# Attention with eight tokens per partition, a list scheduler for the front, and block products for two more operands

## The chip, the cores and the metric

The kernel runs on one core of one Trainium2 chip. The metric is the device time of one execution in microseconds. The kernel before took 1674.87 us (median of 3 runs, 1673.18 to 1677.12).

## The reference

Attention over q, k, v of shape (4, 8, 576, 64), batch, heads, tokens and head size, followed by a mixture of 8 experts over all 2304 tokens with 512 features.

```python
# attention, per batch and head; factor = 4
out_d  = softmax(scale * q_d @ k_d.T) @ v_d      # q_d, k_d, v_d: means over 4 neighbouring tokens (144 rows)
out_up = repeat(out_d, 4)                        # coarse part, repeated for the 4 tokens
mask   = |i - j| < 4                             # local part: 7 neighbours of every token
out    = out_up + softmax(where(mask, scale * q @ k.T, -1e9)) @ v
x      = out, heads side by side                 # (2304, 512)
# experts: every expert sees every token
P = exp(x @ w_gate - max); 8 rounds: rows / row sum, columns / column sum, * 2304 / 8
out = sum over e of P[:, e] * (relu(x @ w1[e]) @ w2[e])   # w1[e] (512, 1024), w2[e] (1024, 512)
```

## The kernel before

**Splitting of numbers.** All large products are made of numbers in two parts, high and low: a high part rounded by ScalarE and a low part, the remainder, by GpSimd or VectorE. A product of two such numbers is three matmuls (high by high, high by low, low by high). Weights arrive as raw tiles `r` of 128x512; `w_convert` (L193) turns each into `w1h`/`w1l` or `w2h`/`w2l`, at L204 and L211 or L214.

**Chunks and pieces.** Four neighbouring tokens are one group, and there are 576 groups. They are cut into six chunks of 64, 64, 128, 128, 128 and 64 groups (L49), that is 256 or 512 tokens. A *piece* is one chunk, or two small chunks side by side. `order` (L1031) lists pairs of a piece and an expert. Each pair has 8 units (`NF`); a unit is `mm1` (L976: 12 matmuls over the piece's tokens into `psh`, then relu into `hh` on ScalarE and the remainder `hl` on VectorE, L991 and L999) and `mm2` (L1004: three matmuls of 512 columns for each tile of 128 tokens into `psy`). The matmuls of the next unit's `mm1` stand ahead of the present unit's `mm2` in TensorE's order. Each unit loads two raw tiles of 256 KB anew.

**The start.** Until the first chunk's x exists, TensorE has no expert work. SyncE (SP) issues loads in a fixed order: q and key windows of the first attention unit (`l_load_q` L233, `l_load_win` L245), the coarse loads `dr` of keys (L423), value windows, `dr` of values, weights. A window holds for 4 tokens the 10 rows that they need; a partition holds one group of 4 tokens of four heads.

**Local attention.** `l_gen` (L276) works through nine units. A unit is 128 groups by four heads. For each head VectorE makes a product `prod` of q and window (L299), a sum over the head size (L322), the softmax over 7 scores (L335 to L355), a product of window and score (L366) and a sum over the window (L397) into `lo`. Three `lo` tiles rotate. For unit 1 alone the q operand and the scores stand in PSUM (`qp`, `scp`); for the others all operands stand in SBUF. In the first unit GpSimd makes five of the eight products.

**Coarse attention.** For the batches after the first, `d_load` reads q, k, v once more, GpSimd sums four tokens (`p_gen` L449, at L473 and L477), and `d_gen` (L627) makes the two products and the softmax for each half of the heads, one after another. `x_gen` (L781) transposes `lo`, adds the coarse output `od` and splits the sum into `xh` and `xl`. A chunk that crosses from one batch to the next needs the coarse output of both.

**The front.** The loop at L1153 places one unit after another, and between them `pump` (L958) places steps of four generators, by a simple clock of each engine: the main chain (`m_gen` L921: coarse attention, x, gate logits, then the gate's rounds `s_gen` L861, all in one chain), the coarse sums, and local attention. As the gate's weights are not known yet, each finished tile of the front is copied to DRAM (`spill`, L1181), and read back later.

**After the front.** The remaining pairs run at L1365, beside them the spilled tiles are read back and added (`back_add`), and `t_gen` (L1256) forms sums of x for the last part. That part handles chunks 3 and 4 (1024 tokens) of all experts by a block product: `m_pair` (L1458) makes a 2x2 block product from 7 products in place of 8. The block part covers `mm1`; its second product (`y_mm`, L1505) is as before. An expert is two halves, each of 84 matmuls in two calls of `m_pair` and 96 in `y_mm`, all of 512 columns.

Of the kernel before, what the change touches and what calls it, by code (L numbers as in the profile page):

```python
# [20 lines left out]
def attention_moe_kernel(  # L21
# [10 lines left out]
    nc = tc.nc  # L32
# [11 lines left out]
    WR = R + 2 * (R - 1)  # L44
# [4 lines left out]
    chunks = [(0, 64), (64, 64)] + [(128 + 128 * i, 128) for i in range(3)] + [(512, 64)]  # L49
# [18 lines left out]
    ps_a = ctx.enter_context(tc.tile_pool(name="ps_a", bufs=2, space=PSUM))  # L68
# [3 lines left out]
    ones = const.tile([128, 128], F32, name="ones")  # L72
    spill = dram.tile([32, 4, 128, DM], F32, name="spill")
# [27 lines left out]
    ap3 = att.enter_context(tc.tile_pool(name="ap3", bufs=3, side="right"))  # L101
    mask = ap1.tile([128, NC, R * W], F32, name="mask")
# [32 lines left out]
    clk = {"pe": 0.0, "dve": 0.0, "act": 0.0, "pool": 0.0, "dma": 0.0}  # L135
    HOP = 0.1

    def at(eng, cost, *deps):
        clk[eng] = max([clk[eng]] + [d + HOP for d in deps]) + cost
        return clk[eng]  # L140

    def dve(n, *deps):
        return at("dve", 0.07 + n / 960.0, *deps)

    def act(n, *deps):
        return at("act", 0.1 + n / 1200.0, *deps)

    def pool(n, *deps):
        return at("pool", 0.02 + n / 420.0, *deps)
# [4 lines left out]

    a_rel = []

    def pa():
        i = len(a_rel)
        a_rel.append(0.0)
        return i, (a_rel[i - 2] if i >= 2 else 0.0)  # L160

    def dma(kb, *deps):

        return at("dma", 0.05 + kb * 0.55, *deps) + 2.0
# [6 lines left out]
    n_dma = [0]  # L171
    n_cv = [0]
    free_t = {}

    def w_load():
        n = n_dma[0]
        if n >= len(units):
            return
        n_dma[0] += 1
        e, f, _ = units[n]  # L180
        r1 = rawp.tile([128, KD, 128], F32, tag="r", name="r1")
        r2 = rawp.tile([128, DM], F32, tag="r", name="r2")
        nc.sync.dma_start(  # L183
            out=r1, in_=moe_w1[e, :, f * 128:(f + 1) * 128].rearrange("(k p) f -> p k f", p=128)
        )
        nc.sync.dma_start(out=r2, in_=moe_w2[e, f * 128:(f + 1) * 128, :])  # L186
        w_raw[n] = (r1, r2, dma(4, clk["pe"], w_ready.get(n - NRAW, 0.0)))

    def w_can(limit, now):
        n = n_cv[0]  # L190
        return n < min(limit, len(units)) and w_raw[n][2] <= now + 0.2

    def w_convert(*deps, need=1e9, low2=nc.gpsimd):  # L193
        n = n_cv[0]
        n_cv[0] += 1
        r1, r2, t_raw = w_raw.pop(n)
        pl = units[n][2]()
        h1 = pl.tile([128, KD, 128], F32R, tag="w1h", name="w1h")
        l1 = pl.tile([128, KD, 128], F32R, tag="w1l", name="w1l")
        h2 = pl.tile([128, DM], F32R, tag="w2h", name="w2h")  # L200
        l2 = pl.tile([128, DM], F32R, tag="w2l", name="w2l")
        done = 0.0
        for r, h, l in ((r1, h1, l1), (r2, h2, l2)):
            nc.scalar.activation(out=h, in_=r, func=AF.Copy)  # L204
            t = act(512, t_raw, *deps)
            t_pool = max(clk["pool"], t) + 1.3
            if r is r2 and can("p", clk["pool"]):
                t_pool += 1
            t_dve = max(clk["dve"], t) + 0.6
            if low2 is nc.gpsimd if r is r2 else t_pool <= max(need, t_dve + 1):  # L210
                nc.gpsimd.tensor_tensor(out=l, in0=r, in1=h.bitcast(F32), op=ALU.subtract)  # L211
                done = max(done, pool(512, t))
            else:
                nc.vector.tensor_tensor(out=l, in0=r, in1=h.bitcast(F32), op=ALU.subtract)  # L214
                done = max(done, dve(512, t))
# [1379 lines left out]
```

## Time and profile before

| | |
|---|---|
| median of 3 runs | 1674.87 us |
| profiled execution, span | 1675.4 us |
| TensorE matmul busy | 1642.7 us (98%), 7941 matmuls |
| VectorE, ScalarE, GpSimd busy | 963.9, 643.8, 936.5 us |
| DMA | 212.75 MB, 127 GB/s on the mean |
| from first expert matmul to the block part | 48.8 to 1012.7 us |
| block part | 1012.7 us to the end |

The span is the time from the first to the last instruction. Busy time of an engine is the union of its instructions' spans; matmuls overlap each other, so the spacing of their starts tells more than their own length. Busy time of an engine that nothing waits for costs nothing. In answers by line, the last column is the idle time of the engine just before the group's instructions, and what ended it.

### The profile page before, as it was taken

The page shows a single profiled execution, that of the slowest core. Times are in us where ns is not written, and L with a number is a line of the kernel's source. Part 1 is how long each engine was busy: PE and PEld are TensorE (multiplying, and loading weights), DVE is VectorE, ACT ScalarE, POOL GpSimd, SP SyncE. Part 2 cuts the span into 40 slices and gives each one's busy share as a digit, 9 for nine tenths or more (in the row PEclk, how much of TensorE's full clock was granted, in tenths as well). Part 3 has the DMA queues.
Part 4 walks back from the last instruction along what each step waited for, and adds up shares of the span by engine and source line. Part 5 has one row for each costly group of instructions (what it writes and reads, how often), then busy time and mean ns, then how long its engine had stood idle before and what let it go on. Part 6 is the DMA issues. An engine that isn't in the chain of part 4 may idle for free.

```text
span 1675.4 us, 22108 instructions
## 1 busy us (share of the span) xinstructions
PE 1642.7 (98%) x7941; PEld 1352.0 (81%) x7941; DVE 963.9 (58%) x1166; ACT 643.8 (38%) x1310; POOL 936.5 (56%) x767
## 2 busy tenths in 40 slices
PE   6989999999999999999999999999999999999999
PEld 5877888888888878788987778888888888888887
DVE  7787853897479678354645554444444444444444
ACT  2554544344444433335653223333333333333332
POOL 6679675777767555444454456544444444444441
PEclk7899999999999999999999999999999999999999
DMA  8877764578476643335557763111111112111111
GB/s 198 200 224 193 197 198 129 144 200 205 140 184 177 154 135 102 116 115 187 189 177 232 222 211 89 51 51 51 51 51 50 51 52 56 53 55 51 51 39 51
DMA packets 221200, 212.75 MB, mean 127 GB/s; under 512 B 12962, under 2 KB 161968, under 8 KB 221090
## 3 DMA queue, kind: packets, MB, share of 16 engines
q1 hardware_dynamic: 211586, 194.04, 42.4%
q10 hardware_dynamic: 9504, 17.31, 2.8%
q8 instruction: 62, 1.02, 0.3%
q14 instruction: 48, 0.39, 0.1%
HBM read 191.37 MB, written 19.92 MB: 126 GB/s over the span
## 4 chain that ended last, share of the span: by engine, by line
PE 50%; DMA 2%; DVE 2%; issue 0%; SPq 0%; POOL 0%; DVEq 0%
PE psm L1438 19%; PE psy L1511 7%; PE psy L1509 7%; PE psy L1510 7%; PE psh L985 5%; DMA s<-spill 2%; PE psy L1011 2%; PE psy L1009 2%; PE psy L1010 2%; DVE acc L1229 1%; DVE hl L999 0%; DVE acc L1224 0%; POOL w2l L211 0%; SPq L186 0%; SPq L183 0%
## 5 line engine op out<-in xcount | busy, mean ns | idle before, releaser
L211 POOL TENSOR_TENSOR w1l<-r,w1h 128x512 fp32r<-128x512 f32 x188 | 260.8, 1387 | 278.3 <-ACT w1h L204 250.4
L211 POOL TENSOR_TENSOR w2l<-r,w2h 128x512 fp32r<-128x512 f32 x156 | 227.7, 1461 | 71.5 <-ACT w2h L204 60.5
L1009 PE MATMUL psy<-w2h,hh 128*128 128x512 f32 x640 | 255.5, 399 | 0.6 <-ACT hh L991 0.6
L1011 PE MATMUL psy<-w2h,hl 128*128 128x512 f32 x640 | 251.1, 392 | 4.3 <-DVE hl L999 3.7
L1010 PE MATMUL psy<-w2l,hh 128*128 128x512 f32 x640 | 250.5, 391 | 0.0
L1353 POOL TENSOR_TENSOR w2l<-r,w2h 128x512 fp32r<-128x512 f32 x64 | 83.2, 1300 | 283.6 <-ACT w2h L1352 283.6
L999 DVE SCALAR_TENSOR_TENSOR hl<-psh,hh 128x512 fp32r<-128x512 f32 (+1 forms) x192 | 114.6, 597 | 193.2 <-ACT hh L991 193.1
L1229 DVE SCALAR_TENSOR_TENSOR acc<-psy,lg,acc 128x512 f32<-128x512 f32 x140 | 103.9, 750 | 200.8 <-PE psy L1511 198.7
L991 ACT ACTIVATE hh<-psh 128x512 fp32r<-128x512 f32 (+1 forms) x192 | 100.7, 525 | 308.2 <-PE psh L985 287.6
L204 ACT ACTIVATE w2h<-r 128x512 fp32r<-128x512 f32 x192 | 120.8, 629 | 183.6 <-POOL w1l L211 83.8
L985 PE MATMUL psh<-xhs,w1l 128*128 128x256 f32 (+1 forms) x512 | 173.6, 339 | 7.4 <-POOL w1l L211 7.4
L985 PE MATMUL psh<-xhs,w1h 128*128 128x256 f32 (+1 forms) x512 | 175.4, 343 | 1.0 <-ACT xhs L816 0.5
L985 PE MATMUL psh<-xls,w1h 128*128 128x256 f32 (+1 forms) x512 | 173.0, 338 | 0.4 <-POOL xls L820 0.4
L1319 POOL TENSOR_TENSOR c1l<-r,c1h 128x512 fp32r<-128x512 f32 (+1 forms) x128 | 144.9, 1158 | 40.4 <-ACT c1h L1316 40.4
L1011 PEld LDWEIGHTS psy<-w2h,hl 128*128 128x128 f32 x640 | 120.5, 188 | 33.7 <-DVE hl L999 7.8
L1009 PEld LDWEIGHTS psy<-w2h,hh 128*128 128x128 f32 x640 | 120.8, 189 | 23.5 <-ACT hh L991 0.8
L1010 PEld LDWEIGHTS psy<-w2l,hh 128*128 128x128 f32 x640 | 120.8, 189 | 21.8
L1316 ACT ACTIVATE c1h<-r 128x512 fp32r<-128x512 f32 (+1 forms) x128 | 64.9, 567 | 173.7 <-POOL r L1324 173.7
L397 DVE TENSOR_REDUCE lo<-prod 128x256 f32<-128x1792 f32 x36 | 123.9, 3443 | 6.6 <-PE psx L798 6.3
L204 ACT ACTIVATE w1h<-r 128x512 fp32r<-128x512 f32 x192 | 119.8, 624 | 11.0 <-ACT sp L1181 6.3
L985 PEld LDWEIGHTS psh<-xhs,w1l 128*128 128x128 f32 x512 | 97.5, 190 | 19.5 <-POOL w1l L211 9.3
L985 PEld LDWEIGHTS psh<-xhs,w1h 128*128 128x128 f32 x512 | 97.5, 190 | 14.4 <-ACT w1h L204 1.2
(188 smaller groups left out, 3578.2 us busy)
## 6 DMA issues: line engine op xcount, KB each, us to landing
r<-in_moe_w_dram SPq DMA_DIRECT2D x512, 256.0 KB
spill<-sp ACTq DMA_DIRECT2D x58, 256.0 KB
s<-spill SPq DMA_DIRECT2D x58, 256.0 KB
dr<-in_k_dram SPq DMA_DIRECT2D x32, 144.0 KB
dr<-in_v_dram SPq DMA_DIRECT2D x32, 144.0 KB
dr<-in_q_dram SPq DMA_DIRECT2D x24, 144.0 KB
lw<-in_v_dram SPq DMA_DIRECT2D x4, 640.0 KB
lw<-in_k_dram SPq DMA_DIRECT2D x2, 1120.0 KB
```

What stands on the lines that cost most here:

```text
L204: nc.scalar.activation(out=h, in_=r, func=AF.Copy)
L211: nc.gpsimd.tensor_tensor(out=l, in0=r, in1=h.bitcast(F32), op=ALU.subtract)
L397: nc.vector.tensor_reduce(out=ot[:, r0:r0 + nr, h % 2], in_=pr[:, r0:r0 + nr].rearrange("p r w d -> p r d w"), axis=AX.X, op=ALU.add,)
L985: nc.tensor.matmul(out=ps, lhsT=w[:, kk], rhs=x[:, kk], start=(i == 0), stop=(i == len(seq) - 1))
L1009: nc.tensor.matmul(out=y, lhsT=hh[:, ts], rhs=h2, start=(f == 0), stop=False)
L1010: nc.tensor.matmul(out=y, lhsT=hh[:, ts], rhs=l2, start=False, stop=False)
L1011: nc.tensor.matmul(out=y, lhsT=hl[:, ts], rhs=h2, start=False, stop=(f == NF - 1))
L1229: nc.vector.scalar_tensor_tensor(out=a, in0=y, scalar=lg[:, tbase[c] + t, e:e + 1], in1=a, op0=ALU.mult, op1=ALU.add)
L1319: nc.gpsimd.tensor_tensor(out=ls[i][:, s], in0=r[:, s], in1=hs[i][:, s].bitcast(F32), op=ALU.subtract)
L1438: nc.tensor.matmul(out=ps, lhsT=wt[:, kk], rhs=xt[:, kk], start=start and j == 0, stop=j == len(seq) - 1, skip_group_check=not start,)
L1509: nc.tensor.matmul(out=y, lhsT=hh[:, f, ts], rhs=h2, start=(f == 0), stop=False)
L1510: nc.tensor.matmul(out=y, lhsT=hh[:, f, ts], rhs=l2, start=False, stop=False)
```

## The change

**Chunks.** Six chunks of 64, 64, 64, 128, 128, 128 groups. A partition of a local attention unit now holds two neighbouring groups (8 tokens) of two heads, with a window of 14 rows in place of 10; a unit is still four (group, head) products of the same shape, in nine units. In the code:

```diff
-    WR = R + 2 * (R - 1)
+    WR = 2 * R + 2 * (R - 1)
-    chunks = [(0, 64), (64, 64)] + [(128 + 128 * i, 128) for i in range(3)] + [(512, 64)]
+    chunks = [(64 * i, 64) for i in range(3)] + [(192 + 128 * i, 128) for i in range(3)]
 def l_parts(c, hh):
...
+        m = n // 2
+        return [
+            (m * i + off // 2, k_ // 2, b, g // 2, (0 if is_small(c) else 4 * hh) + 2 * i)
+            for i in range(128 // m) for off, k_, b, g in segs(t0, n)
+        ]
```

Each load of q or of a window is thus four DMAs or more where it was two or more, and the first unit's windows and q are loaded in two steps of one head slot each (17 DMAs where there were 9). Six `lo` tiles rotate (`NLO`).

**Operands in PSUM.** The scores stand in PSUM (`scp`) for every unit from 1 on, and q too where the running piece has two tiles:

```diff
-            apart = u == 1
+            apart = u >= 1 and alone[0] and (u == 1 or all(
+                len(piece_tiles(order[min(m_next[0] + z, len(units) - 1) // NF][0])) == 2 for z in (0, 8)
+            ))
-            sp = ps_z.tile([128, 4, R, W], F32, tag="y", name="scp") if apart else sc
+            sp = scp if u else sc
```

**Coarse sums from the tiles of local attention.** The second read of q, k and v is left out for the batches after the first. `p_gen` sums four tokens of the tiles that local attention has loaded, `w_gen` writes the sums to DRAM, `e_gen` reads them back in the layout of the coarse attention:

```diff
+        for n, (u, s) in enumerate(s_list):
+            dst = (l_q, l_k, l_v)[s]
+            while u not in dst or n >= len(s_rel) + 2 or (0, n % 2) not in d_taken:
                 yield None
...
+            for h in range(2):
+                nc.gpsimd.tensor_tensor(out=tm[:, h], in0=sv[:, h, :, 0], in1=sv[:, h, :, 1], op=ALU.add)
...
+            nc.gpsimd.tensor_tensor(out=raw[:, 8:12], in0=tv_[:, :, 0], in1=tv_[:, :, 1], op=ALU.add)
```

A tile of unit u+1 is loaded once unit u has read its buffer and the sums have been taken (`ld_gen`).

**x.** `x_gen` makes for a unit and group parity a transposed tile of 512 columns, adds `od` in place in PSUM, and writes half of the tokens of `xh` and `xl` for its features, so a chunk's x is complete only with all its tiles. The low part is always VectorE's.

**The front by a list scheduler.** All work of the front is in generators that say when they are ready, on which engine, for how long, and whether they need the port that VectorE and GpSimd share. `sched` places the step that can start first, ties by rank; weight loads go ahead of other loads, which wait while more than 3 us of transfers are queued:

```diff
+    RANK = {"h": 0, "raw": 0, "x": 1, "r0": 1.1, "r1": 1.2, "d": 1.3, "s": 1, "e": 1, "w": 1, "p": 1.5, "ld": 1.5, "m": 2, "v": 2}
+    def sched(done):
+        while not done():
...
+                st = max(t.ready, clk[t.eng])
+                if t.lock:
+                    st = max(st, clk["port"])
...
+                if best is None or (st, rank) < best[0:2]:
+                    best = (st, rank, nm)
...
+            if isinstance(best[2], str):
+                th[best[2]].step()
```

Low parts of weights go to GpSimd, or to VectorE where GpSimd would be late (`lo_gen`). The front ends at the first unit of a pair after x is complete; the gate's rounds then run beside the pairs that follow. One PSUM bank each serves x (`ps_x`) and coarse attention (`psd`), where two served both.

**Order, and block products for chunks 1, 2 and 3.**

```diff
+        EH = 3
+        order = [((0,), e) for e in range(3)] + [((0, 1), e) for e in range(3, 7)]
+        order += [((2,), 3), ((2,), 4), ((0,), 7), ((3,), 3), ((3,), 4), ((2,), 5), ((3,), 5), ((2,), 6), ((3,), 6), ((3,), 7)]
+        last = [((1, 2), 7)]
+        order += [(p_, e) for e in reversed(range(EH)) for p_ in ((3,), (1, 2))]
...
+        side_f, side_b, side_c, side_d = (1, 2), (3,), (4,), (5,)
+        rest1 = [z for z in order[n_done:] if z[1] >= EH]
+        rest2 = list(last)
+        both = sorted({e for p, e in order[n_done:] if p == side_f and e < EH})
...
+        g1 = plain_part(rest1, n, n + n1, t_gen(side_f, side_b), h_next)
+        while not th["s"].done:
+            th["s"].step()
...
+            blocks_part(side_f, side_b, both, hf_a, hf_b, accp, g1, plain1, reload)
+        g1 = plain_part(rest2, n + n1, len(units), t_gen(side_c, side_d))
...
+        blocks_part(side_c, side_d, range(E), hl_a, hl_b, accc, g1)
```

`rest1` is what the front leaves of experts 3 to 7, `both` what it leaves of experts 0 to 2 on chunks 1, 2 and 3: these go through the block products, the functions of which (`prod`, `m_pair`, `y_mm`) are the same but for their operands. Then one more pair, `((1, 2), 7)`, runs plainly, and the block part on chunks 4 and 5 closes the kernel, as that on 3 and 4 did. Spilled tiles are read back beside the first block part too. During that part the x of chunk 4 lies in DRAM (`xc`), as its buffers hold relu outputs, and is loaded again near its end.

## Rows read from the trace of the kernel before

**Rows 1.** Stretches of the span: length, busy us by engine, granted clock, DMA share, GB/s.
```profile
0.00:48.80 48.80, 33.96 (x256) 25.50 (x256) 35.94 (x47) 12.98 (x39) 31.27 (x23) 0.68 0.90 199
48.80:80.00 31.20, 30.75 (x209) 26.96 (x210) 24.31 (x32) 15.94 (x44) 18.54 (x16) 0.90 0.84 198
80.00:150.00 70.00, 61.80 (x412) 50.89 (x411) 55.38 (x55) 34.77 (x87) 53.10 (x40) 1.00 0.76 207
150.00:650.00 500.00, 500.00 (x2391) 408.22 (x2391) 365.70 (x316) 221.78 (x491) 343.74 (x244) 1.00 0.63 169
```
**Rows 2.** Chain that ended last, in order of time: start, us, what.
```profile
791.35 1.43 PE psh L985 x12
794.16 1.43 PE psh L985 x12
...
954.22 2.72 PE psh L985 x12
959.66 2.72 PE psh L985 x12
...
1054.25 19.38 PE psm L1438 x84
1095.40 19.38 PE psm L1438 x84
```
**Rows 3.** Waits of TensorE: for whom, us in total, times, longest.
```profile
PE psh L985 <- POOL w1l L211: 7.4, 8, 2.0
```
**Rows 4.** Timeline of GpSimd: start, us, what, idle before and what ended it.
```profile
93.12 1.27 POOL L211 TENSOR_TENSOR w1l<-r,w1h 128x512 fp32r<-128x512 f32 x1 [5.05 <-PE psqk L643]
```
**Rows 5.** Timeline of TensorE about 940 us.
```profile
939.42 0.80 PE L1011 MATMUL psy<-w2h,hl 128*128 128x512 f32 x1 [2.98 <-DVE hl L999]
940.02 0.63 PE L1009 MATMUL psy<-w2h,hh 128*128 128x512 f32 x1
```
**Rows 6.** Timeline of TensorE: the first expert matmul.
```profile
48.81 0.58 PE L985 MATMUL psh<-xhs,w1h 128*128 128x256 f32 x1 [0.55 <-ACT xhs L816]
```
**Rows 7.** Timeline of SP's queue at the start.
```profile
2.25 1.83 SPq L255 DMA_DIRECT2D lw<-in_k_dram  x3
...
16.10 11.37 SPq L443 DMA_DIRECT2D dr<-in_v_dram  x8
```
**Rows 8.** VectorE by line, 60 to 690 us: busy us, mean ns, idle before.
```profile
L397 DVE TENSOR_REDUCE lo<-prod 128x256 f32<-128x1792 f32 x32 | 110.9, 3464 | 6.6 <-PE psx L798 6.3
L999 DVE SCALAR_TENSOR_TENSOR hl<-psh,hh 128x512 fp32r<-128x512 f32 (+1 forms) x114 | 72.5, 636 | 129.7 <-ACT hh L991 129.7
L366 DVE TENSOR_TENSOR prod<-lw,sc 128x1792 f32<-128x1792 f32 x28 | 71.2, 2541 | 0.4
L299 DVE TENSOR_TENSOR prod<-lq,lw 128x1792 f32<-128x1792 f32 x28 | 70.2, 2508 | 0.5
L322 DVE TENSOR_REDUCE sc<-prod 128x28 f32<-128x1792 f32 x31 | 62.2, 2007 | 0.1
L366 DVE TENSOR_TENSOR prod<-lw,scp 128x1792 f32<-128x1792 f32 x4 | 8.0, 2012 | 0.0
```
**Rows 9.** Timeline of VectorE: sums into `lo` of units 0, 2 and 8.
```profile
38.69 6.48 DVE L397 TENSOR_REDUCE lo<-prod 128x256 f32<-128x1792 f32 x2
...
228.01 3.47 DVE L397 TENSOR_REDUCE lo<-prod 128x256 f32<-128x1792 f32 x1
...
283.10 3.47 DVE L397 TENSOR_REDUCE lo<-prod 128x256 f32<-128x1792 f32 x1 [0.16 <-PE psx L798]
...
667.17 3.47 DVE L397 TENSOR_REDUCE lo<-prod 128x256 f32<-128x1792 f32 x1
```
**Rows 10.** Timeline of ScalarE: first spill of two pairs of 512 tokens.
```profile
193.35 0.59 ACT L1181 ACTIVATE sp<-psy 128x512 f32<-128x512 f32 x1
...
382.30 0.60 ACT L1181 ACTIVATE sp<-psy 128x512 f32<-128x512 f32 x1
```
**Rows 11.** Line 889, the gate's rounds: ns min/median/max, first to last start.
```profile
L889 DVE TENSOR_REDUCE tmp<-lg x8: 293/303/304, 699.9 to 741.3; 128x18 f32<-128x144 f32 x8
```

More of the change, by code (lines that the diff above doesn't have):

```diff
@@ L187, in w_load, with w_convert @@
[L187 to L193, printed above, removed]
+        return [("p", which, e, f, n) for which in (1, 2)]
+    def w_convert():
         n = n_cv[0]
         n_cv[0] += 1
[L196 to L203, printed above, removed]
-            nc.scalar.activation(out=h, in_=r, func=AF.Copy)
[L205 to L215, printed above, removed]
@@ L455, in p_gen, with e_gen @@
+    def e_gen():
+        for b, hf in halves:
+            if not b:
+                continue
             n = 2 * b + hf
-            if s == 0 and n >= 1 or s == 1 and n >= 3:
-                while halves[n - 1] not in d_taken:
+            for s in (1, 0, 2):
+                us = cover(b, hf)
+                while any((u, s) not in s_out for u in us):
                     yield None
-            if s == 2 and n >= 2:
-                while halves[n - 2] not in od_t:
-                    yield None
@@ L482, in p_gen @@
-            d_sum[b, hf, s] = (t, done)
+                t0 = max(s_out[u, s] for u in us)
+                if s < 2:
+                    while n >= 3 and halves[n - 1] not in d_taken:
+                        yield None
+                    t0 = max(t0, d_done.get(halves[n - 1], 0.0))
+                else:
+                    while halves[n - 2] not in od_t:
+                        yield None
+                    t0 = max(t0, od_t[halves[n - 2]])
+                yield t0 + HOP, "sp", 0.0, False
@@ new lines, in x_gen, with od_ready @@
+        m = n // 2
+        hfs = (0, 1) if is_small(c) else (hh,)
+        p0, np_ = 2 * hfs[0], 2 * len(hfs)
+        bs = sorted({t0 // SD, (t0 + n - 1) // SD})
+        def od_ready(b, hf):
+            return od_f.get(hf) if c == 0 else od_t.get((b, hf))
+        while (u, 2 * a + 1) not in l_done or any(od_ready(b, hf) is None for b in bs for hf in hfs):
+            yield None
+        t_l = max(l_done[u, 2 * a], l_done[u, 2 * a + 1])
+        if c:
+            yield from sx.take()
+            t_l = max(t_l, sx.t)
@@ new lines, in attention_moe_kernel, with s_todo @@
+        rest1 = [z for i, z in enumerate(rest1) if z not in rest1[:i]]
+        del order[n_done:], units[n:]
+        order += rest1 + rest2
+        for c, e in rest1 + rest2:
+            for f in range(NF):
+                units.append((e, f, lambda: wa))
+        n1 = len(rest1) * NF
+        NH = NF // 4
+        def s_todo(es):
+            r = []
+            for e in es:
+                for hf in range(NH):
+                    r += [("s", w_, e, 4 * hf + f, 0) for w_ in (1, 2) for f in range(4)]
+            return r
@@ L1430, in bank @@
             return pl.tile([128, DM], F32, tag=tag, name="psm")
-        def prod(ps, a, b, w, start=True):
-            i, s = w_op[a]
-            wh, wl = w[0][i][:, s], w[1][i][:, s]
-            bh, bl = x_op[b]
-            seq = [z for kk in range(2) for z in ((wh, bh, kk), (wh, bl, kk), (wl, bh, kk))]
-            for j, (wt, xt, kk) in enumerate(seq):
-                nc.tensor.matmul(
-                    out=ps, lhsT=wt[:, kk], rhs=xt[:, kk], start=start and j == 0, stop=j == len(seq) - 1,
-                    skip_group_check=not start,
-                )
```

1548 lines of the change are left out of this document (953 added, 595 removed).

## The prediction, made before the run

> **What bounds the kernel now.** I read the stretches of the span first. From 150 to 650 us TensorE is busy for all 500 us, and between 48.8 and 150 us it misses 0.45 and 8.2 us [rows 1]. So TensorE sets the end almost everywhere, and the reader should ask what its matmuls are spaced by. The chain that ended last gives that. A unit of a 256-token piece starts every 2.81 us (794.16 - 791.35), one of a 512-token piece every 5.44 us (959.66 - 954.22), and a half of an expert in the block part every 41.15 us (1095.40 - 1054.25) [rows 2]. These are 24 matmuls of 512 columns in 5.44 us (0.2267 us each) and 180 in 41.15 us (0.2286 us each).
>
> Next come the losses. TensorE waits 7.4 us for low parts of w1 from GpSimd [rows 3]. These waits are in the first stretch. GpSimd itself was idle there: 5.05 us before 93.12 us, until a coarse product of TensorE had ended [rows 4]. ScalarE and GpSimd lacked raw weights, for SP's queue stood at a coarse load that needed that product's buffer. The clock counts too: 0.90 on the mean over the 31.2 us after 48.8 [rows 1], worth 3.1 us. Late in the plain part there is one larger stall: 2.98 us for `hl`, after which matmuls of 512 columns start 0.60 us apart in place of 0.23 [rows 5]; I count 3.5 us for it. Before 48.81 us nothing of the experts runs at all [rows 6].
>
> **Block products for two more operands (-14.2 us).** Plain, 1024 tokens of one expert are two pieces of 8 units: 16 x 5.44 = 87.0 us. In block products they are two halves: 2 x 41.15 = 82.3 us. For three experts that is 3 x 4.74 = 14.2 us, on TensorE alone, with no stall counted. The number of 256-token units is 64 in both orders (eight pairs), so these cancel. All of it needs `both` to hold three experts, which is weighed below.
>
> A page speaks against this size. The Trainium skill's TensorE: Matmul & The Clock Gate, section Back-to-back issue gap, gives about 131 ns as the sustained spacing for 512 columns. By it 72 matmuls fewer (24 per expert) would be an estimated 9.4 us, and the end 1663 us. The rows show 0.2267 us, not 0.131, so I leave the term at 14.2.
>
> **The first stretch (-7 us).** 24 units of 256 tokens begin the expert work. The coarse reads of q, k and v that stood in SP's order ahead of the weights disappear, and weights go ahead of attention's loads. The loss that this can give back is 0.45 + 8.2 us of idle time; the 3.1 us of the lower clock may come back in part if matmuls follow each other more closely. The bounds are 0 and -11.8. I take -7, near the idle time, for each such unit still asks 2 x 256 KB in 2.81 us, 187 GB/s, of a queue that moved 198 to 207 GB/s here [rows 1].
>
> **The start (+2 us).** The first unit's keys and q take 17 DMAs in place of 9, the value window 5 in place of 3. One costs SP 1.83 / 3 = 0.61 us [rows 7], so ten cost 6.1 us, and everything behind them in that queue, the coarse keys, values and weights, is late by as much if issue is the limit. But two windows are 128 x 2 x 14 x 256 B, 0.92 MB, where they were 1.31 MB: 0.79 MB less, 4.0 us at the 199 GB/s of this stretch [rows 1]. The eight value loads took 1.42 us each to issue (11.37 / 8), over twice 0.61, so the queue was by then limited by bytes, not by issue [rows 7]. Bounds -4.0 and +6.1; I take +2, between them.
>
> **Passages between plain and block parts (+2.5 us).** There is one now, at 3.5 us [rows 5], and there will be three: into the new block part, out of it, and into the last. VectorE has less of the read-back tiles there, since these are added within the new block part too. I take 2 us each, 6 in all against 3.5; bounds 0 and 10.5, that is -3.5 to +7.
>
> **Local attention (0).** Its instructions keep their shapes. What it gains is VectorE's time: from the scores in PSUM, 2.54 to 2.01 us for each product [rows 8], and it no longer waits long for coarse outputs. Three `lo` tiles made unit 2 stop at 231.5 us until 283.1 [rows 9], a hole of 51.6 us in which a whole coarse chain ran. TensorE had work in that time, so on the path this is worth nothing. It decides the two conditions on which the other terms hang.
>
> First, the pace. Units end at 45.2 (38.69 + 6.48) and 670.6 us, eight in 625.4 us: 78.2 us each [rows 9]. VectorE was busy for 24.3 + 55.4 + 365.7 = 445.4 us of 48.8 to 650 us, 7.7 such units, 57.9 each [rows 1]. Of these, 9.0 are relu remainders (72.5 us in 630, 0.115 per us [rows 8]), which go with time. The PSUM scores save 4 x 0.53 = 2.1. So 57.9 - 9.0 - 2.1 = 46.8 us remain per unit, and a VectorE without a pause would need 46.8 / (1 - 0.115) = 52.9 us. With a tenth lost: 58 us. The bounds are 53 and 78.
>
> Second, when TensorE needs chunk 3. A pair of 512 tokens takes 47.2 us in the front (382.30 - 193.35, four pairs [rows 10]); one of 256 tokens by the same ratio 24.5. The first such pair began at 193.3 - 47.2 = 146; now at 141 (+2, -7). Four of them end at 330, three pairs of 256 tokens at 403. Chunk 3 needs the sums of unit 6's values, which are loaded when unit 5 has read its own, and half a coarse chain after that, 25 us by half the hole: 45.2 + 5 x 58 + 25 = 360 us. That leaves 43 us of slack, and no stall up to a pace of 66.6 us. All of x is there at 45.2 + 8 x 58 + 25 = 534 us; the front then ends with the pair that runs, at about 569 us, and three pairs of experts 6 and 7 are left, about 119 us. The gate's rounds started 5.9 us apart [rows 11], eight take 47 us, so they fit beside these. Experts 0 to 2 are untouched: `both` has three.
>
> **Edits at nothing.** The store and second load of chunk 4's x are 2.1 MB each way, 10.5 us at 199 GB/s; the store has the new block part beside it and the load half of a 41.15 us half; without that cover the load's 10.5 us would stand on the path. GpSimd's sums, the writes and reads of the sums, x in place in PSUM and the spills have 500 us of busy TensorE beside them. The transposes and coarse matmuls are the same in columns.
>
> **Sum.** -14.2 - 7 + 2 + 2.5 = -16.7 us on the profiled execution of 1675.4 us: 1658.7. The median of the runs is 0.5 us lower. I predict 1658.
>
> **Rivals.**
> (B) Slower: TensorE runs dry before pair (3, expert 3). If attention keeps its pace of 78.2 us, chunk 3 comes at 461 us where 403 is needed: 58 us of stall, 1716 us. The stall eats the gain of 17 us at a pace of 70.0 us; from there on the kernel is slower. For it: VectorE alone allows no pace under 53 us, so a quarter of its time lost brings it to 70; and a write to DRAM and a read back now stand in the coarse chain. Against it: the hole of 51.6 us, and 43 us of slack.
> (C) The block products come for fewer than three experts, as the front ends late (a pace over 71 us, or TensorE faster than I think): 4.74 us for each, 1663 to 1672 us. It would mean that the change does only part of what it says.
> (D) Loss by 256-token units inside the attention. 24 such units now lose 8.65 us, 0.36 each. In the new order 56 (the first 24, then three pairs, then one) run while VectorE and the loads of attention are at work: 20.2 us if each loses as before, 11.5 more than now in place of 7 less: 1658 + 18.5 = 1677 us. For it: the demand of 187 GB/s, and VectorE's sums of 3.46 us [rows 8], longer than a unit. Against it: the low parts can go to VectorE, and coarse reads are gone.
> (E) The front loses nothing, and the start is limited by bytes: -14.2 - 11.8 - 4.0 + 2.5 gives 1648 us, with free passages 1642.
>
> **How the numbers follow.** My forecast has a chance of 0.50 (own range 1649 to 1668), E 0.14, C 0.10, D 0.12, B 0.14. The range that leaves out 2 in 10 is 1638 to 1684: under it a tenth, over it the worse part of B. A measurement of this kernel tells about 0.2%, 3.4 us, from no change. Faster by more than that: forecast, E, C and near half of D, 0.79; within it 0.05, from D; slower 0.16, B and the rest of D.
>
> **What would show it.** Right: 3960 matmuls of 512 columns in the two block parts and 41.2 us per half in both; TensorE's wait for `w1l` well under 7.4 us; the first expert matmul between 45 and 55 us; units of attention some 58 us apart; three experts in `both`; no stall of over 4 us on TensorE after 150 us. Wrong: a stall on x of chunk 2 or 3 (B), fewer than three experts (C), many waits of 0.3 to 2 us for `hl`, `w1l` or raw weights in units of 256 tokens between 330 and 570 us (D), or a first expert matmul after 55 us.

## The result: slower, 1690.24 us against 1675.71

The changed kernel takes 1690.24 us (median of 4 runs, 1686.39 to 1691.45), the kernel before 1675.71 beside it; the ratio is 1.0081, 95% interval 1.0066 to 1.0096. I had predicted 1658. The profiled execution of the changed kernel has a span of 1684.6 us, that of the kernel before 1675.4: 9.2 us to explain. The trace of the changed kernel is of the fastest of its four runs (1686.39 us), so some 5 us of the 14.5 between the medians stand in no trace.

The stretches of the changed kernel (length, busy us of TensorE, its weight loads, VectorE, ScalarE and GpSimd, granted clock, DMA share, GB/s) answer to [rows 1]:
```profile
0.00:62.10 62.10, 38.78 (x288) 29.53 (x289) 38.30 (x48) 16.89 (x45) 33.56 (x24) 0.64 0.62 156
62.10:80.00 17.90, 17.90 (x125) 16.03 (x125) 16.38 (x22) 11.10 (x32) 10.44 (x9) 0.90 0.71 180
80.00:150.00 70.00, 64.35 (x423) 56.22 (x422) 53.04 (x60) 37.18 (x85) 53.44 (x48) 0.93 0.76 195
150.00:650.00 500.00, 480.78 (x2498) 396.99 (x2497) 391.81 (x421) 239.94 (x538) 301.70 (x248) 0.99 0.62 166
...
732.70:979.10 246.40, 246.40 (x1081) 202.57 (x1080) 140.82 (x189) 78.21 (x141) 127.35 (x115) 1.00 0.30 94
```
Three things differ. The start lasts 62.10 us where it was 48.81 [rows 6], with 156 GB/s in place of 199. From 80 to 150 us the clock is 0.93, not 1.00. From 150 to 650 us TensorE misses 19.2 us; it missed none.

TensorE's first expert matmul, and its waits (for whom, us in total, times, longest), of the changed kernel:
```profile
62.10 0.41 PE L1157 MATMUL psh<-xhs,w1h 128*128 128x256 f32 x1
```
```profile
PE psv L670 <- DMA dr<-in_v_dram: 8.7, 1, 8.7
PE psd L800 <- DVE prod L428: 4.8, 3, 2.3
PE psy L1373 <- DVE hl L1361: 3.5, 2, 1.9
PE psd L800 <- DMA dq<-sums: 3.3, 3, 1.5
PE psd L894 <- DMA dv<-sums: 3.2, 3, 2.8
PE psd L1044 <- DVE stmp L1033: 2.4, 2, 2.1
PE psd L867 <- ACT pt L872: 2.2, 2, 1.8
...
PE psh L1157 <- DVE w1l L1271: 0.4, 1, 0.4
```
The 7.4 us for w1l [rows 3] are gone, as forecast. In their place stand many short waits of attention's and the gate's small matmuls (`psd`), which the planner puts into TensorE's fixed order among the expert matmuls. Each is short, but they add up (the idle time below), and more follows them. These are TensorE's stalls in the front, then stretches of the same kernel:
```profile
96.06 0.34 PE L867 MATMUL psd<-ident,pp 80*72 80x80 f32 x2 [1.82 <-ACT pt L872]
...
130.29 0.29 PE L983 MATMUL psd<-ident,gs 16*128 16x16 f32 x2 [1.97 <-ACT gs L975]
...
282.90 0.25 PE L800 MATMUL psd<-ident,dq 72*128 72x72 f32 x1 [1.54 <-DMA dq<-sums]
...
312.21 0.71 PE L894 MATMUL psd<-pt,dv 72*64 72x144 f32 x2 [2.84 <-DMA dv<-sums]
...
505.12 0.42 PE L800 MATMUL psd<-ident,dq 72*128 72x72 f32 x2 [1.65 <-DVE prod L428]
```
```profile
62.10:65.67 3.57, 3.57 (x17) 3.31 (x17) 3.54 (x4) 1.05 (x3) 1.54 (x2) 0.50 0.88 244
65.67:96.39 30.72, 28.90 (x226) 25.50 (x226) 27.26 (x42) 18.53 (x54) 19.95 (x18) 1.00 0.72 169
96.39:103.21 6.82, 5.53 (x27) 3.83 (x27) 3.63 (x2) 4.45 (x12) 5.55 (x6) 0.50 0.65 219
103.21:130.52 27.31, 24.77 (x170) 22.00 (x167) 19.83 (x17) 14.54 (x32) 18.88 (x18) 1.00 0.78 197
130.52:133.93 3.41, 3.41 (x14) 3.12 (x14) 2.45 (x3) 1.13 (x2) 3.41 (x3) 0.50 0.60 165
284.12:287.53 3.41, 3.41 (x11) 2.64 (x10) 1.58 (x2) 0.86 (x3) 0.00 (x0) 0.50 0.25 85
311.43:318.25 6.82, 5.86 (x24) 4.34 (x25) 0.00 (x0) 0.48 (x2) 1.82 (x2) 0.50 0.51 158
505.99:509.40 3.41, 3.41 (x12) 2.69 (x11) 2.89 (x2) 1.50 (x6) 0.00 (x0) 0.50 0.02 5
```
The granted clock is 0.5 (1.2 GHz) five times behind 90 us, each time at or right behind one of these stalls of 1.5 to 2.9 us. Not every stall brings it: one of 2.26 us at 230 us and three of 1.95, 1.51 and 2.11 at 632 to 646 did not here. Nor does the same stall bring it each time. The one at 230 us stands in e2_two_queues (below) too, and there the clock fell behind it:
```profile
230.86 0.34 PE L800 MATMUL psd<-ident,dq 72*128 72x72 f32 x2 [2.25 <-DVE prod L428]
```
```profile
232.04:235.46 3.42, 3.42 (x13) 2.62 (x12) 2.58 (x2) 0.61 (x3) 0.00 (x0) 0.50 1.02 204
```
So how many stretches of half clock a trace shows is in part a matter of the one execution that was profiled. TensorE works for 25.2 us at half clock behind the first expert matmul (3.57 + 5.53 + 3.41 + 3.41 + 5.86 + 3.41), which loses 12.6 us. Before, it worked for 5.57 us at half clock behind 48.8 us and for 2.87 us about the stall at 939 [rows 5], which lost 4.2 us.

The block parts answer to [rows 2]. The chain of the changed kernel shows their halves by start, duration and count:
```profile
732.88 19.31 PE psm L1826 x84
773.96 19.31 PE psm L1826 x84
...
938.25 19.31 PE psm L1826 x84
979.32 5.44 PE psh L1352 x24
```
Six halves of 41.07 us: three experts were in `both`.

The sum of the 9.2 us: the start +13.3; the block products -14.7 (3 x 87.0, less 246.4); everything else in the plain part +11.5; the last block part -1. For "everything else" I take all time between the first expert matmul and the last block part beyond the units (2.82 and 5.44 us each) and halves: 963.7 - 876.8 = 86.9 us before, 98.4 now. Of these 11.5, the clock is 12.6 - 4.2 = 8.4. TensorE's idle time in this part grew as well, from 14.0 to 24.9 us, which is 10.9. The two together are 7.8 us more than the 11.5. Some 50 small matmuls fewer stand in this part than before, 32 of them since they come ahead of the first expert matmul now (288 matmuls there, 256 before [rows 1]); that this makes up the 7.8 us is not shown.

### The profile page after: what moved, and what is told of

It is laid out like the page before. It is cut to its first block, busy times and chain, and to the rows that moved or that the text cites. A ratio compares the mean times of both kernels' runs of the same rounds, so it can differ in the third digit from the quotient of the medians.

```text
span 1684.6 us, 21871 instructions
## 1 busy us (share of the span) xinstructions
PE 1631.7 (97%) x7845; PEld 1346.0 (80%) x7845; DVE 1006.2 (60%) x1243; ACT 639.9 (38%) x1302; POOL 911.9 (54%) x807
## 4 chain that ended last, share of the span: by engine, by line
PE 79%; DVE 6%; DMA 3%; issue 1%; POOL 1%; ACT 1%; SPq 0%; ACTq 0%; POOLq 0%; DVEq 0%
PE psm L1826 25%; PE psy L1906 9%; PE psy L1907 9%; PE psy L1908 9%; PE psh L1157 8%; PE psh L1352 4%; PE psy L1184 3%; PE psy L1185 2%; PE psy L1186 2%; DVE lo L456 2%; DVE prod L428 2%; PE psy L1371 1%; PE psy L1372 1%; PE psy L1373 1%; DMA lq<-in_q_dram 1%
## 5 line engine op out<-in xcount | busy, mean ns | idle before, releaser
L1908 PE MATMUL psy<-w2h,xl 128*128 128x512 f32 x400 | 155.6, 389 | 0.0
L1826 PE MATMUL psm<-tl,c1h 128*128 128x512 f32 x352 | 138.0, 392 | 0.0
L1826 PE MATMUL psm<-th,c1l 128*128 128x512 f32 x352 | 137.9, 392 | 0.0
L1826 PE MATMUL psm<-th,c1h 128*128 128x512 f32 x352 | 137.9, 392 | 0.0
L1906 PE MATMUL psy<-w2h,xh 128*128 128x512 f32 x352 | 136.9, 389 | 0.0
L1907 PE MATMUL psy<-w2l,xh 128*128 128x512 f32 x352 | 136.9, 389 | 0.0
L1185 PE MATMUL psy<-w2l,hh 128*128 128x512 f32 x336 | 133.5, 397 | 0.0
L1186 PE MATMUL psy<-w2h,hl 128*128 128x512 f32 x336 | 133.1, 396 | 0.0
L1906 PE MATMUL psy<-w2h,xhs 128*128 128x512 f32 x304 | 118.3, 389 | 0.0
L1907 PE MATMUL psy<-w2l,xhs 128*128 128x512 f32 x304 | 118.3, 389 | 0.0
```

The costliest lines, as they stand in the source:

```text
L1185: nc.tensor.matmul(out=ye[z], lhsT=hh[:, ts], rhs=l2, start=False, stop=False)
L1186: nc.tensor.matmul(out=ye[z], lhsT=hl[:, ts], rhs=h2, start=False, stop=(f2 == NF - 1))
L1826: nc.tensor.matmul(out=ps, lhsT=wt[:, kk], rhs=xt[:, kk], start=start and j == 0, stop=j == len(seq) - 1, skip_group_check=not start,)
L1906: nc.tensor.matmul(out=y, lhsT=at_t(h), rhs=h2, start=(f == 0), stop=False)
L1907: nc.tensor.matmul(out=y, lhsT=at_t(h), rhs=l2, start=False, stop=False)
L1908: nc.tensor.matmul(out=y, lhsT=at_t(l), rhs=h2, start=False, stop=(f == 3))
```

## The experiments

**The start: order, queue or loads.** Unit 0's softmax on VectorE now stood at 39.31 us, behind the second coarse maximum (idle 8.71 us), and `psv` on TensorE waited 8.7 us for `dr` of v. e1_late_v:
```diff
-            d_raw[b, hf, p, s] = (t, dma(4 * HK / 128))
+            d_raw[b, hf, p, s] = (t, dma(4 * HK / 128) + (8.0 if n < n_first and s == 2 else 0.0))
```


> The changed kernel, but its planner takes the four raw value tiles of the coarse attention (dr of v) to land 8 us later; that alone puts the softmax of unit 0 ahead of the second coarse maximum in VectorE's order, and the value sums (psv) behind the second pss on TensorE. Theory A (order: of the 13.3 us that the first expert matmul lost, most is VectorE's idle 30.2 to 38.9 us behind the second coarse maximum): softmax of unit 0 at about 30.5 instead of 39.3, the last lo of unit 0 at about 48 instead of 56.7, then psv ends at about 48.6 and pso, od and x follow: first expert matmul at 56 to 58 (62.10 in the changed kernel), total 4 to 6 us down, about 1685. Theory B (loads: the start is bound by what the DMA brings): psv and the value window bind, first expert matmul not below 60, total within 2 us of 1690.

Measured: 1693.28 us, ratio 1.0095 (1.0078 to 1.0112), first expert matmul at 66.01. VectorE and ScalarE of e1_late_v:
```profile
31.55 0.33 DVE L393 SCALAR_TENSOR_TENSOR sc<-sc,mask 128x56 f32<-128x56 f32 x2
...
43.30 0.27 DVE L410 TENSOR_REDUCE mx<-sc 128x16 f32<-128x112 f32 x1 [10.80 <-ACT sc L407]
```
```profile
39.20 0.23 ACT L1464 ACTIVATE wg<-wgr 128x32 fp32r<-128x32 f32 x1 [8.92 <-DMA wgr<-in_moe_w_gate_dram]
```
The softmax came 8 us earlier and then lost all of it: its Exp on ScalarE stood behind `wg`, which waits for a late load. The start is as theory B has it (not below 60 us), the total 3 us above the changed kernel. Order alone gains nothing while loads are late. e2_two_queues:
```diff
-        l_load_win(0, k, l_k, step=1, before=lambda h_a, h_n: l_load_q(0, h_a, h_n))
+        l_load_win(0, k, l_k, step=1, before=lambda h_a, h_n: l_load_q(0, h_a, h_n, nc.scalar))
...
-                nc.sync.dma_start(
+                (nc.scalar if n < 4 else nc.sync).dma_start(
```


> The changed kernel with the order of all engines kept, but the first loads of q and the four raw key tiles are issued by ScalarE instead of SyncE. Theory B (SyncE's queue holds each load until an earlier one has landed, waits of up to 6.6 us): dr of v lands some 5 us earlier, psv starts at 28 to 30 instead of 34.28, first expert matmul at 55 to 58, total 4 to 7 us down. Theory A (VectorE's order alone): the second coarse maximum still stands ahead of the softmax but waits less by as much as psv moves, so the same numbers follow; what tells them apart is e1_late_v. A third: the bytes bind, not the issue, then the rate in 0 to 40 us stays near 150 GB/s and nothing moves by over 1 us.

Measured: 1689.55 us, ratio 1.0071 (1.0051 to 1.0092), no gain; 25 GB/s from 28 to 32 us as in the changed kernel. The edit does less than was expected of it: ScalarE issues the eight loads of q, but the second line stands in a branch that the raw key tiles do not take, and the trace has all eight `dr` of keys still on SyncE, as it has those of values. So taking the q loads off SyncE gains nothing; whether a second queue for what stands behind the value window would, no run shows. Single pieces in the trace gave the next theory: from 27.2 to 32.1 us only pieces of 3584 bytes move, one after the other, 0.144 us each. They belong to a value window of 31 partitions. e7_split31:
```diff
-                    win(p0 + 1, m - 1, b, g + 1, h0, 0, WR)
+                    if u == 0:
+                        win(p0 + 1, 15, b, g + 1, h0, 0, WR)
+                        win(p0 + 16, 16, b, g + 16, h0, 0, WR)
+                    else:
+                        win(p0 + 1, m - 1, b, g + 1, h0, 0, WR)
```


> The changed kernel, but the three window loads of unit 0 that cover 31 partitions are each cut in two, of 15 and of 16 partitions. Nothing else changes, every engine's order is kept. Theory H (a load of 31 partitions of one head or two is moved piece after piece, 3584 bytes in 0.144 us, as by one of the 16 DMA engines alone: 31 pieces from 6.2 to 10.6 us, 62 pieces from 24.7 to 32.6 us at 25 GB/s; SyncE's queue stands behind it for 3.3 and 6.6 us): the rate in 28 to 32 us rises from 25 GB/s to above 120, psq starts at 8 to 9 us instead of 11.3, psv at 24 to 28 instead of 34.3, the first expert matmul at 51 to 55 instead of 62.1, total 7 to 11 us down, about 1681. Rival A (order of VectorE and ScalarE alone): loads come earlier, first expert matmul stays above 58, total within 3 us of 1690.

Measured: 1681.12 us, ratio 1.0031 (1.0018 to 1.0044), 9.1 us under the changed kernel. Two loads are cut, one of keys and one of values, not three: the queue below has one more of each. SyncE's queue (start, us, what; answers to [rows 7]), first of the changed kernel, then of e7_split31 (its later lines stand four further down):
```profile
2.57 1.88 SPq L302 DMA_DIRECT2D lw<-in_k_dram  x5
...
9.62 1.70 SPq L302 DMA_DIRECT2D lw<-in_k_dram  x4
...
14.85 3.55 SPq L302 DMA_DIRECT2D lw<-in_v_dram  x5
19.27 14.02 SPq L527 DMA_DIRECT2D dr<-in_v_dram  x8
```
```profile
6.97 1.81 SPq L302 DMA_DIRECT2D lw<-in_k_dram  x4
...
12.32 5.66 SPq L302 DMA_DIRECT2D lw<-in_v_dram  x6
19.12 6.38 SPq L531 DMA_DIRECT2D dr<-in_v_dram  x8
```
Stretches of the one and the other, and TensorE of e7_split31:
```profile
28.00:32.00 4.00, 0.00 (x0) 0.00 (x0) 2.20 (x5) 0.72 (x2) 0.00 (x0) 0.50 0.06 25
```
```profile
28.00:32.00 4.00, 4.00 (x13) 2.81 (x12) 1.34 (x5) 0.57 (x3) 0.26 (x1) 1.00 1.12 253
```
```profile
26.64 3.66 PE L674 MATMUL psv<-dr,ident 72*72 72x256 f32 x8 [2.62 <-DMA dr<-in_v_dram]
...
54.52 0.41 PE L1161 MATMUL psh<-xhs,w1h 128*128 128x256 f32 x1
```
The same bytes in two loads more: the stretch that moved 25 GB/s moves 253, `psv` begins 7.6 us earlier, the first expert matmul too. (The clock in these two rows is no difference: the clock's records of e7_split31 begin at 55 us, and `psv` matmuls start 0.43 us apart in both.) With the holes gone, order counts: e13, e16 and e18 below bring the first expert matmul to 52.53, 50.95 and 48.92 us; the kernel before had it at 48.81 [rows 6].

**The price of a stall.** e12_two_stalls, in `mm1`:
```diff
+        if n in (len(units) - 6, len(units) - 3):
+            for _ in range(7):
+                nc.scalar.activation(out=h1, in_=h1.bitcast(F32), func=AF.Copy)
```


> The changed kernel, but in the plain stretch of eight ahead of the last block products (979 to 1023 us) ScalarE copies two of the first-matrix tiles seven times in place, so that TensorE waits twice, by about 2.3 us (worked out: hh 0.60, seven copies of 0.52 to 0.62, less the 2.72 us of second-matrix work that covers them). Nothing else of the order changes. Theory K (a stall of this length is followed by a stretch at half clock, and that costs as much again): the clock falls to 0.5 behind each of the two for 3.4 or 6.8 us, and the total rises by 2 x (2.3 + 1.7 to 3.4) = 8 to 11 us. Rival L (the clock falls in the front for another reason, so a stall costs only its own length): no stretch of half clock there, total up by 4 to 5 us.

Measured: 1708.66 us, ratio 1.0187 (1.0159 to 1.0214). The stretch of eight steps took 59.85 us, not 43.55. Stalls and stretches of e12_two_stalls:
```profile
994.32 0.79 PE L1355 MATMUL psh<-xhs,w1h 128*128 128x512 f32 x1 [6.42 <-ACT w1h L1347]
...
1018.88 0.79 PE L1355 MATMUL psh<-xhs,w1h 128*128 128x512 f32 x1 [6.29 <-ACT w1h L1347]
```
```profile
991.05:997.88 6.83, 3.56 (x8) 2.81 (x9) 0.00 (x0) 3.09 (x5) 1.39 (x2) 0.50 0.42 123
997.88:1014.94 17.06, 14.70 (x65) 11.83 (x63) 13.09 (x14) 7.90 (x15) 7.88 (x6) 1.00 0.27 77
1014.94:1021.77 6.83, 2.89 (x7) 2.31 (x8) 2.66 (x5) 3.73 (x6) 0.00 (x0) 0.50 0.13 38
```
The stalls were 6.4 us, not 2.3, since ScalarE's copies also stood behind weights that landed late. Theory K holds, rival L does not: the clock fell both times, in a place where it otherwise stays at 1.00, and 16.3 - 12.7 = 3.6 us are what it cost, 1.8 us a stall. These stalls are over twice as long as those in the front, though, and the clock fell while TensorE still waited; a stall of some 2 us was not forced by itself.

**Fewer stalls.** e4_margin:
```diff
-                    st = max(t.ready + 0.15, clk["pe"])
+                    st = max(t.ready + MARGIN, clk["pe"])      # MARGIN = 1.5
```


> The changed kernel, but its planner puts a small matmul of attention or gating into TensorE's order only 1.5 us after its operands are due (0.15 us in the changed kernel). Theory C (the 19 us that TensorE idles between 150 and 650 us come from small matmuls that were put in too early by a planner whose times run ahead of the chip): that idle time falls to 10 us or less, total 7 to 12 us down, about 1680. Rival D (they come late by much more than 1.5 us, or the idle time is the chain of each tile's own steps): idle time stays above 15 us and the total within 3 us of 1690. Rival E: attention falls behind since each step comes later: units end later, three experts fewer before the gate, total up by 3 us or more.

Measured: 1688.74 us, ratio 1.0065 (1.0040 to 1.0089); the ten runs spread from 1679.78 to 1697.68 us, and the trace is of one of the fastest (1680.83). In this kernel, as in e6_two_experts, the gate of one expert multiplies a few sums that hold two experts already; the instructions are those of the full work. TensorE missed 14.5 us from 150 to 650 us, where it had missed 19.2: by the median nearest to rival D, with neither C's gain nor E's loss; the spread is wider than what C and D differ by.

e8_split31_margin: e7 and e4 together, and `scale_early()` called before the next expert is added.

> The kernel of e7_split31 with the 1.5 us margin of e4_margin besides, and the gate put on the first sums as soon as it is known. Theory K (of the 11.5 us that the front lost, some 10 are TensorE at half clock: 23.9 us at 0.5 in five stretches, each right behind a stall of 1.6 to 3.2 us, against 3.4 us in the kernel before): fewer stalls, at most three stretches of half clock behind 70 us, total 10 to 16 us under the changed kernel, 1674 to 1680. Rival E (attention that comes later costs an expert in the front): the split's gain alone or less, 1681 or more.

Measured: 1678.92 us, ratio 1.0016 (1.0000 to 1.0033); first expert matmul at 53.20 us; four stretches of half clock behind 70 us, 17.1 us in all. Within the range named, though one stretch more. The 2.2 us under e7 alone are not clear of the spread of the runs (1675.52 to 1685.66 here, 1678.60 to 1686.94 there).

e5_probs_sbuf:
```diff
-            sp = scp if u else sc
+            sp = sc
```


> The changed kernel, but the probabilities of units 1 to 8 stay in SBUF instead of standing in the PSUM tile that TensorE's small matmuls write (psd). TensorE's order is the same in every instruction. Theory F (sharing the tile makes the psqk transposes wait for VectorE's products, 4.8 us in 3 stalls, and similar short ones): these waits go, total 4 to 6 us down. Rival G: the products (2.00 to 2.03 us) now read both operands from SBUF and share the port with GpSimd: the w1l and w2l subtractions on GpSimd (1.1 to 1.3 us each) wait, products last 2.0 to 2.6 us, w1l stalls on TensorE come back, total up by 2 to 8 us.

Measured: 1702.29 us, ratio 1.0144 (1.0117 to 1.0170). VectorE by line, 60 to 620 us, of the changed kernel and of e5_probs_sbuf:
```profile
L428 DVE TENSOR_TENSOR prod<-lw,psd 128x1792 f32<-128x1792 f32 x32 | 64.5, 2015 | 5.8 <-ACT kz L814 3.4 <-PE psd L894 1.7
```
```profile
L428 DVE TENSOR_TENSOR prod<-lw,sc 128x1792 f32<-128x1792 f32 x32 | 79.0, 2468 | 0.6
```
Rival G: 0.45 us more a product, 14.5 us of VectorE. The waits for `prod` go, and those for `dq` (9.4 us) and `dv` (4.9) grow. The waits for w1l came to 1.3 us in all, so the loss took another route than G's: attention is late (the last `lo` ends at 598.3 us, not 581.2), and TensorE's order waits for it.

e6_two_experts:
```diff
-        EH = 3
+        EH = 2
...
+        order += [((3,), 2), ((1, 2), 2)]
```


> The changed kernel, but two experts instead of three take their block products for tokens of both sides; the third is done plainly, 16 steps of 5.44 us = 87.0 us instead of two halves of 41.07 = 82.1. Theory M (the block products save 4.9 us an expert, as measured in the changed kernel): total up by 4 to 6 us. Rival N (the passages between plain and block parts give back what they save): total unchanged or down.

Measured: 1687.88 us, ratio 1.0068 (1.0046 to 1.0090). The total is 2.4 us under the changed kernel, as rival N has it (unchanged or down), and not M's 4 to 6 us above. The block part shrank by 82.2 us (246.43 to 164.27), as M says, but the plain part ahead of it grew by 82.2 us too (670.6 to 752.8), not by 87.0. The changed kernel's stalls of 2.0, 1.5 and 2.1 us at 632 to 646 us (two for `hl`, one for `stmp`, beside the gate's rounds) are not there: other pieces stand beside the gate, and TensorE's idle time in that part is 20.0 us, not 24.9. So the products save 4.9 us an expert by their own length, and stalls that hang on which piece runs beside the gate can outweigh it.

**Toward a version that beats both.** e13_late_loads, in `dma`, on top of e8:
```diff
-        clk["dma"] = max(clk["dma"], clk["sp"] + 0.6) + 0.05 + kb * 0.55
+        clk["dma"] = max(clk["dma"], clk["sp"] + 0.6, 4.0) + 0.05 + kb * (0.55 if th else 0.75)
```


> The kernel of e8_split31_margin, and its planner reckons the loads of the start as late as the trace has them (first bytes at 4 us, 36% more time a byte), so that the four score reductions and the softmax of unit 0 come ahead of the second coarse maximum on VectorE. Theory A again (with the 31-partition loads gone, VectorE's order is what holds the start: idle 16.95 to 24.16 us and 28.7 to 30.0 us in e8_split31_margin): lo of unit 0 done at 40 to 44 us instead of 47.7, first expert matmul 48 to 51 instead of 53.2, total 2 to 5 us under e8_split31_margin, 1674 to 1677. Rival (the coarse side, od at 44.5 us, binds next): first expert matmul 51 to 53, total within 2 us of 1679.

Measured: 1675.86 us, ratio 0.9999 (0.9980 to 1.0018); last `lo` of unit 0 at 47.1, first expert matmul at 52.53. The softmax came earlier, Exp then waited on ScalarE behind the first value sums: theory A's total, but its rival's start. e14_margin_07 has MARGIN 0.7, e15_hop_03 has HOP 0.3.

> The kernel of e13_late_loads with a margin of 0.7 us instead of 1.5. If stalls behind 60 us are set by how late the small matmuls' operands are against the plan (1 to 4 us), 0.7 us leaves more of them: 20 to 25 us at half clock instead of 17, total 2 to 4 us above e13_late_loads. If the margin itself delays attention, total 1 to 4 us below.

> The kernel of e13_late_loads whose planner also reckons 0.3 us instead of 0.1 us from one engine to another. If the remaining stalls of 1 to 4 us (139.6 xls, 283 psd, 397 spill, 515 sums) come from a plan that runs ahead of the chip everywhere, they shrink: half clock behind 70 us under 12 us, total 2 to 5 us below e13_late_loads. If they come from single misjudged steps (a load, a shared tile), no change beyond 2 us.

Measured: e14 1676.17 us, 0.9992 (0.9980 to 1.0005), 23.9 us at half clock behind 70 us (e13: 17.1) but the same time, as neither side of its expectation has it; e15 1696.33 us, 1.0115 (1.0092 to 1.0139), 37.5 us of half clock behind 70 us, not under 12: that theory fell, and its rival (no change beyond 2 us) too.

The last four correct single steps. e16_late_v2 adds 5 us to the landing of `dr` of v; e19_sums_gate, on top of it with MARGIN 0.7:
```diff
-                    t_in = dma(1)
+                    t_in = dma(1) + 2.5
...
-        pump(t, 0.0)
         nc.vector.scalar_tensor_tensor(
             out=hl, in0=ps, scalar=0.0, in1=hh.bitcast(F32), op0=ALU.max, op1=ALU.subtract
         )
-        return hh, hl, dve(nt, t_h)
+        t_h = dve(nt, t_h)
+        pump(t, 0.0); return hh, hl, t_h
```
e17_all_07 besides, and e18_all_15 the same with MARGIN 1.5:
```diff
-            self.t = t
+            self.t = max(self.t, t)
...
-                    t_v = pv_prod(h, nc.vector, pr)
+                    t_v = pv_prod(h, nc.vector, pr); sd.t = max(sd.t, t_v) if u else 0.0
```


> The kernel of e13_late_loads, and its planner takes the raw value tiles of the coarse attention to land 5 us later still, so that ScalarE's Exp of unit 0 stands ahead of the first eviction of value sums (in e13_late_loads it waited from 25.9 to 29.9 us behind one that waited for dr of v). Theory A: lo of unit 0 done at 43 to 44 us instead of 47.0, first expert matmul at 48.5 to 50 instead of 52.5, total 2 to 4 us down, 1672 to 1674. Rival (coarse side binds): od comes at 46 us or later since the value sums moved behind, first expert matmul 51 to 53, total as e13_late_loads.

> e16_late_v2 with a margin of 0.7 us, and the planner corrected in three places: the re-read sums land 2.5 us later than it took them to; a small matmul that writes the PSUM tile shared with the probabilities waits for VectorE's last product from it; and in the plain stretch the hl of a step goes ahead of the gate's rounds. Theory K (each stall of 1.6 us or more costs itself and 1.7 us of clock): of the nine stalls of over 2 us in e14_margin_07, five by dq or dv of sums, two by the products, two by the gate, at most three are left, half clock behind 70 us at most 10 us (23.9 there), total 1664 to 1670. Rival E (each correction only delays attention, and the time is lost there): total 1674 to 1680.

> The same with a margin of 1.5 us. If the margin is still needed beside the three corrections: 2 to 4 us below e17_all_07. If it only delays attention: equal or up to 4 us above.

> e17_all_07 without the correction for the shared PSUM tile. If the shared tile's stalls matter (two of over 2 us in e14_margin_07): 4 to 8 us above e17_all_07; if not: within 2 us.

Measured: e16 1674.77 us, 0.9989 (0.9972 to 1.0007), with the last `lo` of unit 0 at 44.1 us and the first expert matmul at 50.95, a little behind the 48.5 to 50 of theory A; e17 1673.01, 0.9975 (0.9965 to 0.9986); e18 1685.01, 1.0045 (1.0033 to 1.0057); e19 1691.05, 1.0078 (1.0065 to 1.0092). e17_all_07 is faster than both kernels, 17 us under the changed one, though not the 1664 to 1670 expected. Half clock behind 70 us is 13.6 us. The waits for re-read sums fell from 12.3 us in e14_margin_07 to 1.1, but those for `prod`, which another correction meant to remove, rose from 4.2 to 11.3. TensorE's waits from 50 to 620 us, and a stretch, of e17_all_07:
```profile
PE psd L804 <- DVE prod L432: 7.6, 5, 2.7
PE psd L871 <- DVE prod L432: 2.8, 1, 2.8
```
```profile
150.00:650.00 500.00, 479.30 (x2483) 394.90 (x2482) 397.35 (x423) 239.04 (x534) 307.63 (x252) 0.99 0.62 164
```
TensorE still misses 20.7 us there. From the first expert matmul to the block part e17_all_07 takes 668.2 us, the changed kernel 670.6. So most of what it gained is the start (50.65 us in place of 62.10), and no run took the stalls out of the front.

e19 does not tell what the shared tile costs, for one stall elsewhere outweighs it. TensorE of e19_sums_gate, and two stretches:
```profile
420.40 0.95 PE L898 MATMUL psd<-pt,dv 72*64 72x144 f32 x5 [13.62 <-DMA dv<-sums]
```
```profile
408.12:420.00 11.88, 0.00 (x0) 0.00 (x0) 7.43 (x4) 0.93 (x2) 8.51 (x5) 0.50 0.51 140
420.00:435.42 15.42, 10.38 (x37) 6.12 (x38) 10.18 (x17) 1.90 (x4) 0.51 (x2) 0.50 0.45 94
```
GpSimd waited 2.7 us for a value window, worked on low parts of weights between its two sums, and the read back of `dv` was issued at 417 us, after TensorE's order had come to its matmul. e18 has one of 8.7 us at the same place. Which of the single corrections is worth how much stays open; each shifts the whole list.

## Why the prediction was wrong

**The start (+2 us, bounds -4.0 and +6.1)** is the first step that failed: +13.3 us. I counted the loads and their bytes, not how a load spreads over the DMA engines. Splitting two loads of 31 partitions gave 7.6 us of the start and 9.1 us of the total back; the planner's order gave the rest of the start (48.92 us in e18_all_15). I read "the queue was by then limited by bytes, not by issue" off [rows 7], from a kernel whose first window is cut as 1 + 63 partitions, and carried it over to 1 + 31.

The Trainium skill would have said so: its DMA: Bandwidth & Descriptors, section Why a DMA increments its semaphore by 16 and not by 1, tells that a load uses as many DMA engines as the largest number up to 16 that divides the slowest dimension of both its sides. That is one for 31 partitions, 15 and 16 for the halves. The trace agrees: pieces one by one at 25 GB/s, and 253 GB/s in that stretch once they are split.

**The first stretch (-7 us)** came out at about 0. The waits for w1l went, 7.4 to 0.4 us, and TensorE's idle time up to 150 us fell from 8.65 to 5.65 us; but work at half clock there rose to 3.57 + 5.53 + 3.41 = 12.5 us, a loss of 6.3 us where it was 2.8. For the front behind 150 us there was no term at all, and that is the second step that failed: from 150 to 650 us TensorE idled for 19.2 us and lost 6.3 us more to half clock, where it had lost neither. I priced only what left. The planner's fixed order of TensorE puts each small matmul of attention at a time that it reckons, and when VectorE, ScalarE or a re-read sum is 1 to 3 us later than that, all expert work behind it waits; I had "500 us of busy TensorE beside them" for it. Five of these stalls came with a stretch of half clock; the clock cost 8.4 us more than before, and e12_two_stalls shows that such a stretch costs time beyond the stall. That the fixed order is at fault is read from the traces: no run takes it away, and which part of the change makes the operands late stays open.

**Block products (-14.2 us)** were right: 14.7 by the halves of 41.07 us, and three experts in `both`. The sustained spacing of the Trainium skill's TensorE: Matmul & The Clock Gate, section Back-to-back issue gap, which I weighed against it, would have given an estimated 9.4. The trace does not agree with it (5.44 us for 24 matmuls), and the measurement decides.

**Passages (+2.5)** cost nothing: the eight steps between the block parts took 43.55 us, 8 x 5.44.

**Local attention (0)**: a unit took (581.2 - 56.7) / 8 = 65.6 us, not 58, yet under the 66.6 at which I let stalls begin, and TensorE never ran dry for chunk 3. The pace is where it also shows: `lo` of the last unit ended at 581.2 us where I had all of x at 534. Rival B is thus not what happened, nor C. Rival D was nearest (1677 us, small losses in many places), yet with the wrong place: the waits are at `psd`, in pieces of either size, not at `hl`, `w1l` or raw weights of 256-token units.

Of what I had named as the signs of a wrong forecast, one came true: the first expert matmul after 55 us.

## What to carry to other kernels

Before pricing loads by bytes or by issues, look at the partition count of each: a load of 31 partitions held the whole queue here while DMA moved 25 GB/s. When a list scheduler fixes the order of the engine that bounds the kernel, ask how late each small operand can be against the plan, and price a stall there with the stretch at half clock that can come with it (1.8 us for each of two forced stalls of 6.4 us), not by its own length alone. A gain by counting (4.9 us an expert) came out in the block parts as reckoned, but what the new plan did to the start and to the front outweighed it.

## What the runs showed of the hardware that I had not expected

- A load of 62 pieces of 3584 bytes on 31 partitions moved at 25 GB/s (0.144 us a piece); with that load cut into 15 and 16 partitions the same stretch moved 253 GB/s. Issuing the q loads from a second engine did not change it (25 GB/s from 28 to 32 us again).
- The granted clock fell to 0.5 about single stalls of 1.5 to 2.9 us, though not about all of them, and the same stall at 230 us (2.26 and 2.25 us) brought it in one execution and not in another; about two forced ones of 6.4 us it fell while TensorE still waited, and what it cost was only the work done before it rose (1.8 us each).
- Products with one operand in PSUM took 2.02 us on the mean and 2.00 to 2.03 each, with both in SBUF 2.47 on the mean and 2.01 to 3.13 each. Those 0.45 us, 32 times on an engine that does not set the end, came with a kernel 12 us slower, in which attention came late to its places in TensorE's order.
- The same corrections at two margins, 0.7 and 1.5 us, differ by 12 us (1673.01 and 1685.01): a plan made by greedy steps is not smooth in its parameters.
